# Chunk 0's gate and up projections with the tokens stationary on centred x, and merged DMA transposes, in a fused state-space and SwiGLU kernel

## The chip, the cores and the metric

The kernel runs on one core of one Trainium2 chip. The metric is device microseconds of one launch: 181.08 us, the median of three runs (180.85 to 181.24). Engines: TensorE (PE, with its weight loads PEld), VectorE (DVE), ScalarE (ACT), GpSimd (POOL), SyncE (SP, which here only issues DMAs; SPq is its queue).

## What is computed

The input x has 2048 tokens of 512 features, in bf16. It is layer-normalised, and two branches work on the result:

```python
xn = layernorm(x)                                       # over the 512 features, eps 1e-5
# A: diagonal complex state space, 512 states
Bu = xn @ B_bar.T                                       # B_bar = ((Lam_bar - 1) / Lam) * B
h[t] = Lam_bar * h[t-1] + Bu[t]
A = 2 * real(h @ C.T) + xn * Dskip
# B: SwiGLU, 1376 hidden
B = (silu(xn @ w_gate) * (xn @ w_up)) @ w_down
out = x + A + B
```

## The kernel before

Tokens go in four chunks of 512 (`CW`), each of four tiles of 128; hidden columns in ten tiles of 128 and one of 96 (`FT` = 11). Every matmul of the projections has weights stationary and the transposed, normalised input `xnT` (features on partitions, 512 tokens) moving, four feature blocks (`KD`) per product. All engines run their instructions in the order in which the program writes them (`manual_schedule`), so the order is set by hand: TensorE's stream is written out, and DVE's and ACT's pieces of the state-space work stand in a backlog of (cost, operation) pairs from which `pump(us)` takes what fits beside the matmuls just written; `need(tag)` flushes a stage. A wait of one instruction holds all that stand behind it on its engine, and on SyncE's queue too.

**Head** (lines 120 to 154 loads, 612 to 659). SyncE loads x tile 0, halves of the first gate group, x tile 2, halves of the up group, x tile 3, and so on; ACT's queue loads x tile 1. Weights come in three groups of hidden tiles, 3, 4 and 3 (`fgroups`, line 89). Ten dummy matmuls of 512 columns on a zeroed tile keep TensorE busy meanwhile. Each x tile of chunk 0 goes through statistics on DVE (`ln_stats`, 182), rstd by Ln and Exp on ACT (193), normalising on DVE (`norm_dve`, 205), four transposes on TensorE and a copy from PSUM (`xT_pe`, 215), and then `head_mm` (603) makes three gate and three up tiles for those 128 tokens at once, with 128 moving columns. After the last x tile the parameters of the state space follow: a transpose, exponentials on ACT, a table load, and small sines (`params_a`, `params_a2`, `params_sin`).

**Chunk 0, rest.** Hidden tiles 3 to 6 (line 700), the B projection of the state space (`bproj_tile`, 347; `BT` holds B transposed), hidden tiles 7 to 10. Meanwhile DVE computes statistics and normalised tiles of chunk 1 and sine and cosine tables (`table_ops`, 257). Later chunks get `xnT` by a DMA transpose of each normalised tile (`xT_dma`, 225: 128x512 each). B and C are transposed by DMAs of 128 columns, eight each (lines 139 and 723).

**A chunk in general.** `bproj_chunk(c)`, `gateup_chunk(c)`; ACT drains PSUM (`gu_out` with silu, line 441, and copy, 442; the B projection's copy, 354), DVE multiplies gate and up in pairs (446), rotates, scans (394) and rotates back to `wt`, and computes `CF` from C (338); `out_chunk(c)` has 44 matmuls with w_down (514) and 32 with `CF` (524) into the same banks. Eight PSUM banks go round. `out_chunk(0)` comes after chunk 2's B projection, and so on; the last chunk's results leave through DVE and SyncE (527).

Of the kernel before, what the change touches and what calls it, by code (L numbers as in the profile page):

```python
# [10 lines left out]
F32 = mybir.dt.float32  # L11
# [12 lines left out]
def kernel(  # L24
# [62 lines left out]
    xnT = const.tile([128, KD, L], BF16, name="xnT")  # L87

    fgroups = [(0, 3), (3, 7), (7, FT - 1)]
# [26 lines left out]
    def load_w1_half(tiles, view, gi, k0, k1):  # L116
        a, b = fgroups[gi]
        nc.sync.dma_start(out=tiles[gi][:, k0:k1, :], in_=view[:, k0:k1, a * 128:min(F, b * 128)])  # L118

    nc.sync.dma_start(out=xall[:, 0, :], in_=x_v[:, 0, :])  # L120
    nc.vector.memset(xall[:, 1, 0:2], 0.0)
    nc.scalar.dma_start(out=xall[:, 1, :], in_=x_v[:, 1, :])
# [8 lines left out]
    load_w1(nc.sync, wu_g, wu_v, 1)  # L131
# [5 lines left out]
    for part, src in enumerate((A_B_re, A_B_im)):  # L137
        for k in range(KD):
            nc.sync.dma_start_transpose(out=BT[:, part, k, :], in_=src[:, k * 128:(k + 1) * 128])
        if part == 0:  # L140
            load_w1(nc.sync, wg_g, wg_v, 2)
            load_w1(nc.sync, wu_g, wu_v, 2)

    nc.sync.dma_start(out=w_last[:, :, 0:LB], in_=wg_v[:, :, FL + LA:F])
    nc.sync.dma_start(out=w_last[:, :, LB:LB + LA], in_=wg_v[:, :, FL:FL + LA])
    nc.sync.dma_start(out=w_last[:, :, LB + LA:128], in_=wu_v[:, :, FL:FL + LA])

    def load_late():
        nc.sync.dma_start(out=wu_last[:], in_=wu_v[:, :, FL + LA:F])
        nc.sync.dma_start(out=xall[:, 2 * TPC:NT, :], in_=x_v[:, 2 * TPC:NT, :])  # L150
        nc.sync.dma_start(out=wd_sb[:, 0:nfull, :], in_=B_w_down[0:nfull * 128, :].rearrange("(k p) d -> p k d", p=128))
        if nfull < FT:
            nc.sync.dma_start(out=wd_sb[0:LB, nfull, :], in_=B_w_down[FL + LA:F, :])
            nc.sync.dma_start(out=wd_sb[LB:LB + LA, nfull, :], in_=B_w_down[FL:FL + LA, :])
# [9 lines left out]
    nc.vector.memset(eps_t[:], EPS)
    ident = const.tile([128, 128], BF16, name="ident")
    make_identity(nc, ident[:])
# [24 lines left out]
    lnv = const.tile([128, TPC], F32, name="lnv")  # L191

    def ln_rstd_act(n):
        nc.scalar.activation(out=lnv[:, n:n + 1], in_=mv[:, n, 1:2], func=ACT.Ln, bias=eps_t[:])
        nc.scalar.activation(out=rstd[:, n:n + 1], in_=lnv[:, n:n + 1], func=ACT.Exp, scale=-0.5)

# [8 lines left out]
    def norm_dve(n, lo=0, hi=D):  # L205
        c, i = divmod(n, TPC)
        nc.vector.tensor_scalar(out=xn_tile(c)[:, i, lo:hi], in0=xall[:, n, lo:hi], scalar1=mv[:, n, 0:1],  # L207
                                scalar2=rstd[:, n:n + 1], op0=ALU.subtract, op1=ALU.mult)

    def norm_act(n):  # L210
        c, i = divmod(n, TPC)
        nc.scalar.activation(out=xn_tile(c)[:, i, :], in_=xall[:, n, :], func=ACT.Identity,
                             scale=rstd[:, n:n + 1], bias=nb[:, n:n + 1])

    def xT_pe(n, k0=0, k1=KD, on_dve=False):
        c, i = divmod(n, TPC)
        tp = bank((128, KD, 128), BF16)
        for k in range(k0, k1):
            nc.tensor.transpose(out=tp[:, k, :], in_=xn_tile(c)[:, i, k * 128:(k + 1) * 128], identity=ident[:])  # L219
        if on_dve:  # L220
            nc.vector.tensor_copy(out=xnT[:, k0:k1, n * 128:(n + 1) * 128], in_=tp[:, k0:k1, :])
        else:
            nc.scalar.copy(out=xnT[:, k0:k1, n * 128:(n + 1) * 128], in_=tp[:, k0:k1, :])

    def xT_dma(n):
        c, i = divmod(n, TPC)
        nc.sync.dma_start_transpose(out=xnT[:, :, n * 128:(n + 1) * 128], in_=xn_tile(c)[:, i, :])


# [12 lines left out]
    def prm_transpose():  # L242
        pp = bank((128, 128), BF16)
        nc.tensor.transpose(out=pp[:], in_=prm_rows[:], identity=ident[:])
        return pp

    def params_a(pp):
        V.tensor_copy(out=prm[:].rearrange("p t q -> p (t q)"), in_=pp[:, 0:3 * NQ])
        nc.scalar.activation(out=dt_t[:], in_=ldt, func=ACT.Exp)

    def params_a2():
        V.tensor_tensor(out=dre[:], in0=dt_t[:], in1=lre, op=ALU.mult)
        nc.scalar.activation(out=r_t[:], in_=dre[:], func=ACT.Exp)
        nc.scalar.preload_act_table_set("silu_and_others")
# [529 lines left out]
```

## Time and profile before

| | us |
|---|---|
| median of three runs | 181.08 |
| lowest and highest | 180.85, 181.24 |
| profiled execution | 181.21 |
| its span, first to last instruction | 179.4 |
| granted TensorE clock in it | 0.999 |

The span is 1.8 us shorter than the time of the same execution. Rows of the timeline read: start, duration (both us), engine, line, operation, what it writes `<-` what it reads, count, and in brackets the idle time before it and what ended that. In a merged row the duration covers all of its instructions, and a matmul's end is modelled with the array's latency, so spacings are read from starts. Rows of groups read: busy us, mean ns of one. In tables of stretches the columns are the length, the busy time of PE, PEld, DVE, ACT and POOL, the granted clock, the DMA engines' busy share and GB/s.

### The profile page before, as it was taken

The page shows a single profiled execution, that of the slowest core. Times are in us where ns is not written, and L with a number is a line of the kernel's source. Part 1 is how long each engine was busy: PE and PEld are TensorE (multiplying, and loading weights), DVE is VectorE, ACT ScalarE, POOL GpSimd, SP SyncE. Part 2 cuts the span into 40 slices and gives each one's busy share as a digit, 9 for nine tenths or more (in the row PEclk, how much of TensorE's full clock was granted, in tenths as well). Part 3 has the DMA queues.
Part 4 walks back from the last instruction along what each step waited for, and adds up shares of the span by engine and source line. Part 5 has one row for each costly group of instructions (what it writes and reads, how often), then busy time and mean ns, then how long its engine had stood idle before and what let it go on. Part 6 is the DMA issues. An engine that isn't in the chain of part 4 may idle for free.

```text
span 179.4 us, 2491 instructions
## 1 busy us (share of the span) xinstructions
PE 173.4 (97%) x908; PEld 83.4 (46%) x924; DVE 155.0 (86%) x248; ACT 104.8 (58%) x190; POOL 23.4 (13%) x30
## 2 busy tenths in 40 slices
PE   7899999999999999999999999999999999999993
PEld 2684444443444444444444444444444444444742
DVE  3649998799999999999999999999999986996033
ACT  3459956998299959022799661024866949805000
POOL 7001100000500000025400000014000004315000
PEclk9999999999999999999999999999999999999999
DMA  5999757994036600011840000007300007964512
GB/s 147 294 263 210 163 98 177 357 190 109 5 72 168 252 4 0 0 11 22 112 93 2 0 0 4 0 0 80 37 0 5 0 0 109 139 103 45 76 58 61
DMA packets 28492, 15.53 MB, mean 87 GB/s; under 512 B 18336, under 2 KB 28416, under 8 KB 28448
## 3 DMA queue, kind: packets, MB, share of 16 engines
q1 hardware_dynamic: 24592, 11.87, 28.5%
q0 software_dynamic: 3456, 3.28, 14.4%
q10 hardware_dynamic: 432, 0.23, 0.4%
q8 instruction: 7, 0.11, 0.3%
q14 instruction: 5, 0.04, 0.1%
HBM read 8.03 MB, written 5.24 MB: 74 GB/s over the span
## 4 chain that ended last, share of the span: by engine, by line
PE 93%; DMA 2%; SPq 1%; DVE 1%; issue 1%
PE ps L427 36%; PE ps L514 21%; PE ps L352 15%; PE ps L524 15%; DMA xall<-in_A_x_dram 2%; PE ps L609 2%; PE ps L453 2%; PE ps L463 1%; SPq L118 1%; DVE stats L183 0%; PE ps L219 0%; SPq L126 0%; SPq L120 0%; DVE xn L207 0%; DVE xall L527 0%
## 5 line engine op out<-in xcount | busy, mean ns | idle before, releaser
L514 PE MATMUL ps<-wd_sb,guT 128*128 128x512 bf16 (+4 forms) x195 | 38.6, 355 | 0.2
L427 PE MATMUL ps<-xnT,wg 128*128 128x512 bf16 x143 | 37.6, 379 | 0.3
L427 PE MATMUL ps<-xnT,wu 128*128 128x512 bf16 x146 | 37.5, 379 | 0.1
L394 DVE TENSOR_TENSOR_SCAN g<-r_t,car,u 128x512 bf16<-128x512 f32 x24 | 28.9, 1263 | 0.0
L524 PE MATMUL ps<-CF,wt 128*128 128x512 bf16 (+2 forms) x140 | 28.1, 355 | 0.2
L352 PE MATMUL ps<-xnT,BT 128*128 128x512 bf16 x126 | 28.2, 379 | 0.1
L514 PEld LDWEIGHTS <-guT 128*128 128x128 bf16 (+1 forms) x198 | 18.5, 98 | 19.9
L441 ACT ACTIVATE guT<-ps 128x512 bf16<-128x512 f32 x40 | 25.2, 629 | 2.5 <-PE ps L427 2.3
L442 ACT CAST u<-ps 128x512 bf16<-128x512 f32 x40 | 24.7, 618 | 2.7 <-PE ps L427 2.7
L427 PEld LDWEIGHTS <-wu 128*128 128x128 bf16 x148 | 14.5, 98 | 17.5
L427 PEld LDWEIGHTS <-wg 128*128 128x128 bf16 x148 | 14.3, 98 | 17.6 <-issue 0.8
L530 ACT CAST res<-ps 128x512 bf16<-128x512 f32 x12 | 6.8, 582 | 23.5 <-PE ps L524 23.5
L524 PEld LDWEIGHTS <-wt 128*128 128x128 bf16 x144 | 13.4, 98 | 14.3
L531 POOL DMA_DIRECT2D out_dram<-res x12 | 10.5, 1033 | 72.6 <-ACT res L530 67.5
L352 PEld LDWEIGHTS <-BT 128*128 128x128 bf16 x128 | 12.5, 98 | 15.1
L354 ACT CAST u<-ps 128x512 bf16<-128x512 f32 x32 | 17.7, 614 | 2.4 <-PE ps L352 2.2
L486 ACT ACTIVATE xr<-xall,nb,rstd 128x512 bf16<-128x512 bf16 x16 | 12.0, 808 | 8.4 <-DVE xall L492 5.9
L183 DVE BATCH_NORM_STATS2 stats<-xall 128x6 f32<-128x512 bf16 x16 | 10.7, 671 | 3.2 <-DMA xall<-in_A_x_dram 3.2
L446 DVE TENSOR_TENSOR guT<-guT,u 128x1024 bf16<-128x1024 bf16 x20 | 13.5, 679 | 0.0
L527 DVE TENSOR_TENSOR xall<-ps,xall 128x512 bf16<-128x512 f32 (+2 forms) x6 | 3.1, 514 | 9.1 <-PE ps L524 9.1
L199 POOL TENSOR_TENSOR rstd<-ve,neg_half 128x4 f32<-128x4 f32 x3 | 5.3, 1751 | 43.6 <-DVE ve L198 43.6
L362 DVE TENSOR_TENSOR pm<-u,c 128x2048 bf16<-128x2048 bf16 x8 | 9.8, 1221 | 1.2 <-ACT c L279 1.1
(101 smaller groups left out, 169.0 us busy)
## 6 DMA issues: line engine op xcount, KB each, us to landing
out_dram<-in_A_x_dram SPq DMA_DIRECT2D x1, 1536.0 KB, 8.7
out_dram<-res POOLq DMA_DIRECT2D x12, 128.0 KB, 3.2
out_dram<-xall POOLq DMA_DIRECT2D x3, 512.0 KB, 5.7
wd_sb<-in_B_w_down_dram SPq DMA_DIRECT2D x1, 1280.0 KB, 10.1
xall<-in_A_x_dram SPq DMA_DIRECT2D x1, 1024.0 KB, 5.9
wg<-in_B_w_gate_dram SPq DMA_DIRECT2D x1, 512.0 KB, 6.1
wu<-in_B_w_up_dram SPq DMA_DIRECT2D x1, 512.0 KB, 7.1
xall<-in_A_x_dram SPq DMA_DIRECT2D x1, 512.0 KB, 7.9
```

The costliest lines, as they stand in the source:

```text
L183: nc.vector.bn_stats(out=stats[:, n, 0, :], in_=xall[:, n, :])
L352: nc.tensor.matmul(ps[:], lhsT=BT[:, part, k, q * 128:(q + 1) * 128], rhs=xnT[:, k, c * CW:(c + 1) * CW], start=(k == 0), stop=(k == KD - 1))
L354: nc.scalar.copy(out=u_tiles[c][:, part, q, :], in_=ps[:])
L394: V.tensor_tensor_scan(out=g()[:, part, q, :], data0=r_t[:, q:q + 1].to_broadcast([128, CW]), data1=u_tiles[c][:, part, q, :], initial=ini ...
L427: nc.tensor.matmul(ps[:fs, lo:hi], lhsT=wslice(groups, fi, k), rhs=xnT[:, k, c * CW + lo:c * CW + hi], start=(k == 0), stop=(k == KD - 1))
L441: nc.scalar.activation(out=guT[:fs, fi, :], in_=psg[:fs], func=ACT.Silu)
L442: nc.scalar.copy(out=u_pair[c][:fs, fi % 2, :], in_=psu[:fs])
L446: products.append(lambda: V.tensor_tensor(out=g, in0=g, in1=u, op=ALU.mult))
L486: nc.scalar.activation(out=box["xr"][:], in_=xall[:, n, :], func=ACT.Identity, scale=rstd[:, n:n + 1], bias=nb[:, n:n + 1])
L514: nc.tensor.matmul(o[:], lhsT=gu_tiles[c][:fsz[fi], fi, i * 128:(i + 1) * 128], rhs=wd_sb[:fsz[fi], fi, lo:hi], start=(fi == 0), stop=False)
L524: nc.tensor.matmul(o[:], lhsT=w_tiles[c][:, part, q, i * 128:(i + 1) * 128], rhs=CF[:, part, q, lo:hi], start=False, stop=(part == 1 and q ...
L531: nc.gpsimd.dma_start(out=out_v[:, n, lo:hi], in_=res[:, lo:hi], accum_op=ALU.add)
```

## The change

1. **Chunk 0's gate and up.** Hidden groups are now 4, 4 and 2 tiles. For chunk 0 the tokens are stationary (`xcT`, 128 tokens of centred x, not yet scaled) and the weights move: 512 columns of one group (256 in the last) for one token tile. The row scale rstd comes in the drains (`sw_out`), where tokens are on partitions. The product silu(gate)*up is made token by token in `g0` (in chunk 1's buffer `guT`) and comes to the hidden-major layout by two DMA transposes (`g0_dma`).
2. **Centring.** Tiles 0 and 1 are transposed uncentred by matmuls with the identity, and -mean is added in PSUM by a matmul of a constant matrix (-1/512) with diag(sum of each row); the sums come from DVE (tile 0) and ACT (tile 1). Tiles 2 and 3 are centred on DVE ahead of their transpose. rstd of chunk 0 is a power on POOL, one for each tile; the exponentials of the parameters too. The first ACT table load is gone; silu's comes at the start.
3. **xnT of chunk 0** (only the B projection and the last hidden tile need it) is normalised on DVE and transposed by DMA.
4. **DMA transposes are merged**: one for each chunk's `xnT` (512x512), one for each part of B and of C.
5. **Order.** ACT's queue loads a quarter of the first gate group and half of the first up group. Chunk 1's statistics and normalising stand ahead of most of the tables on DVE; the last hidden tile of chunk 0 comes after its B projection; 4 wide and 3 narrow dummies stand ahead, on a constant of ones that is set at the start.

```diff
-    fgroups = [(0, 3), (3, 7), (7, FT - 1)]
+    fgroups = [(0, 4), (4, 8), (8, FT - 1)]
...
     nc.scalar.dma_start(out=xall[:, 1, :], in_=x_v[:, 1, :])
-    nc.scalar.preload_act_table_set("natural_log_exp_and_others")
-    load_w1_half(wg_g, wg_v, 0, 0, KD // 2)
-    load_w1_half(wg_g, wg_v, 0, KD // 2, KD)
+    load_w1_half(nc.sync, wg_g, wg_v, 0, 0, HK)
+    nc.scalar.preload_act_table_set("silu_and_others")
+    load_w1_half(nc.scalar, wg_g, wg_v, 0, HK, HK + 1)
+    load_w1_half(nc.sync, wg_g, wg_v, 0, HK + 1, KD)
+    load_w1_half(nc.scalar, wu_g, wu_v, 0, 0, HK)
     nc.sync.dma_start(out=xall[:, 2, :], in_=x_v[:, 2, :])
-    load_w1_half(wu_g, wu_v, 0, 0, KD // 2)
-    load_w1_half(wu_g, wu_v, 0, KD // 2, KD)
+    load_w1_half(nc.sync, wu_g, wu_v, 0, HK, KD)
     nc.sync.dma_start(out=xall[:, 3, :], in_=x_v[:, 3, :])
...
-        for k in range(KD):
-            nc.sync.dma_start_transpose(out=BT[:, part, k, :], in_=src[:, k * 128:(k + 1) * 128])
+        nc.sync.dma_start_transpose(out=BT[:, part], in_=src[:, :])
...
+    def diag_dve(i):
+        nc.vector.tensor_scalar(out=diag[:, i, :], in0=ident[:], scalar1=sums[:, i:i + 1], scalar2=None, op0=ALU.mult)
...
+    def cT_mm(ps, src, k, first, stop):
+        nc.tensor.matmul(ps[:, k * 128:(k + 1) * 128], lhsT=src[:, k * 128:(k + 1) * 128], rhs=ident[:], start=first, stop=stop)
+
+    def cT_mean(ps, i, k0, k1):
+        nc.tensor.matmul(ps[:, k0 * 128:k1 * 128], lhsT=minus_mean[:],
+                         rhs=diag[:, i:i + 1, :].to_broadcast([128, k1 - k0, 128]), start=False, stop=True)
...
-    def xT_dma(n):
-        c, i = divmod(n, TPC)
-        nc.sync.dma_start_transpose(out=xnT[:, :, n * 128:(n + 1) * 128], in_=xn_tile(c)[:, i, :])
+    def xT_dma(c):
+        nc.sync.dma_start_transpose(out=runs(xnT[:, c]), in_=xn_tile(c)[:].rearrange("p k i d -> p (k i d)"))
...
+    def sw_mm(ps, groups, gi, i, k0=0, k1=KD):
+        a, b = fgroups[gi]
+        for k in range(k0, k1):
+            nc.tensor.matmul(ps[:, 0:(b - a) * 128], lhsT=xcT[:, k, i * 128:(i + 1) * 128], rhs=groups[gi][:, k, :],
+                             start=(k == 0), stop=(k == KD - 1))
+
+    def sw_out(gi, i, psg, psu):
...
+        nc.scalar.activation(out=g0[:, a:b, i, :], in_=by_k(psg[:, 0:w]), func=ACT.Silu, scale=scale)
+        nc.scalar.activation(out=u_pair[0, gi][:, i % 2, 0:w], in_=psu[:, 0:w], func=ACT.Copy, scale=scale)
...
+    def g0_dma(a, b):
+        nc.sync.dma_start_transpose(out=runs(gu_tiles[0][:, a:b, :]), in_=g0[:, a:b].rearrange("p f i d -> p (f i d)"))
...
-    dummy(10, CW)
-    ln_stats(0)
-    ln_rstd_act(0)
+    dummy(warm, 4, CW)
+    dummy(warm, 3, 128)
+    sum_dve(0)
+    sum_act(1)
+    diag_dve(0)
...
+    head_mm(0, 0)
+    ln_stats(1)
+    mean_act(2)
+    ln_rstd(1, 2)
+    head_mm(0, 1)
+    ln_stats_half(0, 0)
+    center(2, mean2[:])
+    ln_stats_half(0, 1)
+    ln_rstd(0, 1)
+    head_mm(1, 0)
...
+    for n in range(TPC):
+        norm_dve(n)
+    xT_dma(0)
+    params_a()
+    load_bt(1)
+    load_last()
+    load_late()
...
+    need("ln0")
     for part in range(2):
         for q in range(NQ):
             bproj_tile(0, part, q)
...
+    need("ln1")
+    g0_dma(0, fgroups[1][1])
+    g0_dma(fgroups[1][1], FT - 1)
+    load_down()
+    gateup_last(0)
```

`head_mm(which, i)` is gate (0) or up (1) of group 0 for token tile i. In the changed program SyncE's queue is: x tile 0, a gate half and a quarter, x tile 2, an up half, x tile 3, groups 1 and 2, x of chunk 1, B's first transpose, `xnT` of chunk 0, B's second, four small weight loads, x of chunks 2 and 3, `xnT` of chunk 1, the two product transposes (32 and 8 blocks of 128x128), w_down, C's two, `xnT` of chunk 2. Of the DMAs from SyncE and ACT together each waits until the one eight places earlier has landed.

More of the change, by code (lines that the diff above doesn't have):

```diff
@@ L211, in norm_act @@
         c, i = divmod(n, TPC)
-        nc.scalar.activation(out=xn_tile(c)[:, i, :], in_=xall[:, n, :], func=ACT.Identity,
+        nc.scalar.activation(out=xn_tile(c)[:, :, i, :], in_=by_k(xall[:, n, :]), func=ACT.Identity,
                              scale=rstd[:, n:n + 1], bias=nb[:, n:n + 1])
-    def xT_pe(n, k0=0, k1=KD, on_dve=False):
-        c, i = divmod(n, TPC)
[L217 to L223, printed above, removed]
@@ L576, with dummy @@
     BP = 4 * 0.2163
[L577 to L579 removed]
+    one = nc.const_aps.tensor(1.0, (128, 1), BF16)
+    def dummy(ps, n, cols):
         for _ in range(n):
[L581 removed]
+            nc.tensor.matmul(ps[:, 0:cols], lhsT=one.to_broadcast([128, 128]), rhs=one.to_broadcast([128, cols]),
+                             start=True, stop=True)
     def ln_rest(c, on_act):
@@ L593, in one @@
                 (norm_act if on_act else norm_dve)(n)
[L594 removed]
+                if n % TPC == TPC - 1:
+                    xT_dma(c)
             tail.append((0.05 if on_act else 0.35, one))
         return ops, tail
[L600 to L610 removed]
@@ L612 @@
[L612 to L636 removed]
+    G, U = wg_g, wu_g
@@ new lines, in head_mm @@
+    def head_mm(which, i, k0=0, k1=KD):
+        if held[i][which] is None:
+            held[i][which] = bank()
+        sw_mm(held[i][which], (G, U)[which], 0, i, k0, k1)
+    dummy(warm, 4, CW)
[3 more added lines that the diff above has]
+    diag_dve(0)
+    for k in range(KD):
+        cT_mm(p0 if k < HK else p1, xall[:, 0, :], k, k % HK == 0, False)
+    for k in range(KD):
+        cT_mm(p2 if k < HK else p3, xall[:, 1, :], k, k % HK == 0, False)
+    dummy(warm, 1, 128)
+    cT_mean(p0, 0, 0, HK)
```

233 lines of the change are left out of this document (128 added, 105 removed).

## The prediction

> **What bounds the kernel now.** I read the busy shares and the chain first, then the timeline of the first 14 us, then the DMA queue of SyncE (SPq), since the change touches the head and the transfers.
>
> ```profile
> PE 173.4 (97%) x908; PEld 83.4 (46%) x924; DVE 155.0 (86%) x248; ACT 104.8 (58%) x190; POOL 23.4 (13%) x30
> PE 93%; DMA 2%; SPq 1%; DVE 1%; issue 1%
> ```
>
> TensorE is the bound: 97% busy, 93% of the chain. Time can be gained only where it waits, and that is the head. The timeline there:
>
> ```profile
> 1.23 4.19 PE L581 MATMUL ps<-junk 128*128 128x512 bf16 x10 [1.23 <-DVE eps_t L164]
> 3.04 0.69 DVE L183 BATCH_NORM_STATS2 stats<-xall 128x6 f32<-128x512 bf16 x1 [1.85 <-DMA xall<-in_A_x_dram]
> 5.25 0.28 PE L219 MATMUL ps<-ident,xn 128*128 128x128 bf16 x2
> 5.99 0.50 PE L609 MATMUL ps<-xnT,wg 128*128 128x128 bf16 x6 [0.18 <-ACT xnT L223]
> 6.27 0.69 DVE L183 BATCH_NORM_STATS2 stats<-xall 128x6 f32<-128x512 bf16 x1 [0.52 <-DMA xall<-in_A_x_dram]
> 6.83 0.34 PEld L609 LDWEIGHTS <-wu 128*128 128x128 bf16 x6 [0.30 <-DMA wu<-in_B_w_up_dram]
> 8.04 0.69 DVE L183 BATCH_NORM_STATS2 stats<-xall 128x6 f32<-128x512 bf16 x1 [0.86 <-DMA xall<-in_A_x_dram]
> 9.31 0.40 PE L219 MATMUL ps<-ident,xn 128*128 128x128 bf16 x4 [0.63 <-DVE xn L207]
> 10.38 0.83 PE L609 MATMUL ps<-xnT,wg 128*128 128x128 bf16 x12
> 11.04 0.39 PE L219 MATMUL ps<-ident,xn 128*128 128x128 bf16 x4
> 13.28 1.03 PE L427 MATMUL ps<-xnT,wg 128*128 128x512 bf16 x3
> ```
>
> x tile 0 is there at 3.04, the first useful product starts at 5.99, and TensorE then waits for wu (0.30) and for the late x tile 2 (0.63). From 13.28 on it runs without a gap:
>
> ```profile
> 33.14 7.07 PE L352 MATMUL ps<-xnT,BT 128*128 128x512 bf16 x31
> 59.27 7.07 PE L352 MATMUL ps<-xnT,BT 128*128 128x512 bf16 x32
> 66.17 9.68 PE L514 MATMUL ps<-wd_sb,guT 128*128 128x512 bf16 x43
> 75.69 7.07 PE L524 MATMUL ps<-CF,wt 128*128 128x512 bf16 x31
> ```
>
> Thirty-two wide matmuls take 66.17 - 59.27 = 6.90, or 0.216 each; a narrow one (128 columns) takes (11.04 - 10.38)/12 = 0.055. TensorE's streamed columns hardly change: gate and up of chunk 0 stay 80 wide matmuls' worth, the transposes stay 16 narrow ones, and the mean adds four of 256 columns ahead of the first product. So the result is the shift of the head, plus any wait that opens later.
>
> **The head.** By 13.28 the kernel before has made 96 narrow matmuls, the worth of 24 wide ones. The new group 0 is 32 wide ones; the kernel before gets that far at 13.28 + 8 x 0.216 = 15.0. When does the new one (call it H)? The durations:
>
> ```profile
> L223 ACT COPY xnT<-ps 128x256 bf16<-128x256 bf16 x2 | 0.7, 372 | 0.3 <-PE ps L219 0.3
> L212 ACT ACTIVATE xn<-xall,nb,rstd 128x512 bf16<-128x512 bf16 x8 | 6.5, 821 | 6.2 <-DVE nb L202 6.2
> L207 DVE TENSOR_SCALAR xn<-xall,mv,rstd 128x512 bf16<-128x512 bf16 x7 | 2.6, 405 | 0.4 <-ACT rstd L195 0.3
> L199 POOL TENSOR_TENSOR rstd<-ve,neg_half 128x4 f32<-128x4 f32 x3 | 5.3, 1751 | 43.6 <-DVE ve L198 43.6
> ```
>
> The plain sum of tile 0 on DVE isn't in the trace; I price it like the statistics (0.69), bounded by a 512-wide elementwise operation (0.41) and twice the statistics. With the diagonal (0.2, an estimate from the 0.41 row at a quarter of the width), the mean matmul (0.2) and the copy (0.37), half of tile 0 stands at 4.5; ACT's half follows its sum of tile 1 (0.82), its diagonal and its copy, at about 5.1. So data are ready 0.9 sooner than 5.99. Then weights set the pace: they now come in 512-column groups, 1024 KB instead of 768 KB.
>
> ```profile
> 0.00:2.00 2.00, 0.77 (x2) 0.28 (x3) 0.35 (x4) 0.69 (x1) 1.10 (x7) 1.00 0.11 14
> 2.00:4.00 2.00, 2.00 (x6) 0.76 (x5) 0.93 (x3) 0.61 (x2) 1.93 (x5) 1.00 0.93 273
> 4.00:6.00 2.00, 1.82 (x12) 0.84 (x11) 1.61 (x5) 1.41 (x6) 0.15 (x1) 1.00 0.92 232
> 6.00:8.00 2.00, 1.87 (x31) 1.70 (x31) 0.88 (x2) 1.20 (x4) 0.00 (x0) 1.00 1.00 302
> 1.20 0.93 SPq L118 DMA_DIRECT2D wg<-in_B_w_gate_dram  x2
> DMA to landing us min/median/max: 2.7/4.4/6.1
> ```
>
> The GB/s, the last figure of the first four rows, sum to 28, 574, 1038 and 1642 KB at 2, 4, 6 and 8 us. x tile 2 was the end of the first 768 KB, moved by 4.8 and seen at 6.27; x tile 3 the end of 1280 KB, moved by 6.8 and seen at 8.04: 1.2 to 1.4 from move to use. The wu wait ended 1.2 after its 960 KB. The first wg half, issued at 1.20, is the end of 448 KB, moved by 3.5 and landed after 2.7, at 3.9: only 0.4. I take 0.9 and keep 0.4 and 1.4. Group 0's gate is complete after 768 KB (both x tiles and 512): 4.8 + 0.9 = 5.7. Its up halves come at 1280 and 1408 KB: 6.8 and 7.2, plus 0.9. So: gate of tiles 0 and 1 from 5.1, ending 5.7 + 6 x 0.216 = 7.0; up of tile 0 from 7.7, its second half from 8.1, done at 8.55; then 20 wide matmuls (4.3), 8 narrow transposes and the parameters' (0.5), and about 0.25 for tile 3, whose statistics and centring stand behind its landing. **H = 13.6**, a gain of **1.4**. Without any weight wait H = 5.1 + 6.9 + 0.5 = 12.5 (gain 2.5); with 1.4 for landing, 14.0 (gain 1.0).
>
> This lets ACT's queue, which issues a quarter of gate and half of up after its table load, share the engines with SPq; if the transfers went in issue order, the gate's third quarter would come behind 1152 KB and H would be 14.05. [...]
>
> **What is hidden.** Draining by tokens adds a per-row scale to ACT's drains, but 16 wide and 8 half ones are some 13 us (0.6 and 0.4 each) beside 17 us of matmuls. The rstds and both exponentials go to POOL; five stand ahead of the sines, one after the other at up to 1.75, from about 6.2 on: rstd of the last tile at 13 to 14, dt at 14.5 to 16. ACT's sines stand ahead of the drain of tile 2 and hold it till 15.4 to 16.8; TensorE wants that drain's PSUM bank at about 17.5. Hidden; if POOL is slower still, it costs up to 0.5. DVE's backlog begins with the statistics of chunk 1 and reaches CF, which the first state-space outputs need, after 58.4 us:
>
> ```profile
> 13.56 0.68 DVE L183 BATCH_NORM_STATS2 stats<-xall 128x6 f32<-128x512 bf16 x1
> 66.79 4.05 DVE L338 SCALAR_TENSOR_TENSOR CF<-CT,nc2im,cm 128x512 bf16<-128x512 bf16 x6
> 71.17 0.75 DVE L338 SCALAR_TENSOR_TENSOR CF<-CT,nc2im,cm 128x512 bf16<-128x512 bf16 x1 [0.33 <-ACT cm L335]
> ```
>
> The same operations now start after the sines' arguments, at 15.9 to 17.3, so CF ends at 74.3 to 75.7. TensorE will want the eighth CF row at 75.7 (below). Covered, with 0 to 1.4 to spare; what goes beyond is paid in full.
>
> **SyncE's queue decides.** The transposes become fewer instructions but more data: chunk 0's xnT (4 blocks of 128x512) and the product g*u (10 blocks) are new on this queue.
>
> ```profile
> 5.90 7.27 SPq L139 DMA_TRANSPOSE BT<-in_A_B_re_dram  x4
> 15.02 5.09 SPq L139 DMA_TRANSPOSE BT<-in_A_B_im_dram  x4
> 27.79 0.50 SPq L150 DMA_DIRECT2D xall<-in_A_x_dram  x1
> 28.34 0.58 SPq L151 DMA_DIRECT2D wd_sb<-in_B_w_down_dram  x1
> 28.96 2.60 SPq L153 DMA_DIRECT2D wd_sb<-in_B_w_down_dram  x1
> 31.61 0.57 SPq L154 DMA_DIRECT2D wd_sb<-in_B_w_down_dram  x1
> 32.23 6.43 SPq L723 DMA_TRANSPOSE CT<-in_A_C_re_dram  x4
> L227 SPq DMA_TRANSPOSE xnT<-xn x12: 1188/1219/1283, 21.9 to 91.5; - x12
> DMA to landing us min/median/max: 2.4/2.4/3.7
> ```
>
> A block costs SyncE 1.22 and lands 1.2 after its issue ends. No row shows a merged one. Call M the price of four blocks in one instruction: 1.2 if all of it is per instruction, 4.9 if all is per block. Plain DMAs of 1024 and 1280 KB take 0.50 and 0.58, so I take 0.5 of the 1.22 as fixed and 0.72 per block: M = 0.5 + 4 x 0.72 = **3.4**, and keep both ends. [...]
>
> - xnT of chunk 1: BT's first transpose can't start before the last up half is there (8.5) and then waits for room as before (7.27 - 5.09 = 2.2). Behind it come xnT of chunk 0, BT's second, five small loads (2.7) and xnT of chunk 1: landed at 8.5 + 2.2 + 4M + 2.7 + 1.2 = 14.6 + 4M, that is 28.2, or 4.6 after DVE has normalised chunk 1 (26.3 to 27.5 by my count of its queue): 30.9 to 32.1. TensorE wants it at H + 6.9 (group 1) + 3.5 (group 2) + 6.9 (B projection) + 0.9 = 31.8. Just in time; in the kernel before this point is 33.14.
> - xnT of chunk 2: after that the ten product blocks (2.5M), the three wd loads (0.58 + 2.60 + 0.57, 3.8), CT (2M, and 1.2 of waiting as in its row) and itself: landed at 19.6 + 9.5M = 51.9. ACT's normalising of chunk 2 must end by 53; by its place behind four drains of chunk 1 it ends at about 50. Wanted at 31.8 + 6.9 + 1.8 + 17.3 = 57.8, against 59.27 before. The first state-space output follows at 57.8 + 6.9 + 9.5 = 74.2 (before: 75.69), the eighth CF row 1.5 later.
>
> **The sum.** Head 1.4 earlier, all else in TensorE's order unchanged: 181.21 of the profiled execution (span 179.4 and 1.8 around it) - 1.4 = 179.8. That execution lies 0.13 above the median of the three runs, 181.08, so I say **179.7**.
>
> **The rivals.**
> - *The transposes are dear (slower).* M from 4.2 on: xnT of chunk 2 then lands after 59.5, more than 1.5 behind its need, and all of the gain is gone. At M = 4.9 it lands at 66.2, a wait of 8.4: 181.1 - 1.4 + 8.4 = 188. For it: in the trace every block costs 1.2 alike, from HBM or SBUF. Against: plain DMAs show a fixed part. Chance 0.24.
> - *The clock opens later.* Ten dummies at 0.42 each, then 0.055 for 128 columns (cold would be 0.105): in this trace the clock opened after some 4 us of dense work, by 5.25. The new kernel gives it 2 us of dummies and then transposes with gaps. If it needs another stretch of that length, gate of tiles 0 and 1 runs at 0.42: done at 8.65 instead of 7.0, and up begins then, not at 7.7: 1.0 lost, 180.7. Chance 0.09. [...]
> - *DVE or POOL runs late.* POOL operations above 1.75 push the sines, DVE's backlog and CF behind their cover: 0.5 to 1.0 lost, 180.2 to 180.7. Chance 0.10.
> - *The weights come at once.* Gain 2.5, then held at about 2.4 by xnT of chunk 1: 178.6. Chance 0.07.
> - The forecast, 178.9 to 180.4: chance 0.50.
>
> A difference below 0.2% (0.36 us) can't be told from none in a measurement of this kernel. Faster: 0.50 + 0.07, and 0.10 of the two middle rivals: 0.67; within: 0.09; slower: 0.24. The range goes from 178.4, below the fastest case, to 183.0, into the dear transposes, and leaves out some 0.17 of theirs and little below.
>
> **What would show it.** First matmul from xcT at about 5.1, group 0 done by 13.6; matmuls of 512 columns 0.216 apart from there; no wait of TensorE ahead of the B projections of chunks 1 and 2; a merged 512x512 transpose near 3.4 on SyncE; CF done by 75.7. I am wrong if SyncE shows more than 4.2 for it, if TensorE is still at half clock after 6, or if gate and up weights land after 9.

## The result and the profile after

| | before | after |
|---|---|---|
| median, us | 180.91 (180.81 to 181.24, 8 runs) | **179.94** (179.04 to 180.57, 8 runs) |
| ratio, 95% interval | | 0.9941 (0.9915 to 0.9966) |
| profiled execution, its span | 181.21, 179.4 | 179.48, 177.5 |
| group 0 of chunk 0 done (before: 32 wide matmuls' worth) | 15.0 | 13.40 |
| B projection of chunks 1, 2 starts | 33.14, 59.27 | 31.57, 57.70 |
| first state-space output | 75.69 | 74.12 |

The change is faster by 0.6%. Its median falls into a gap: four of the eight times lie at 179.04 to 179.59, four at 180.28 to 180.57, and the profile is of the lower four. The shares and the chain of the page of after, as for before:

```profile
PE 172.8 (97%) x852; PEld 82.1 (46%) x868; DVE 157.7 (89%) x258; ACT 109.2 (61%) x188; POOL 26.7 (15%) x36
PE 92%; DMA 3%; DVE 1%; SPq 1%; issue 1%; ACT 0%
```

TensorE is the bound as before. Its timeline, first the head and then the later stages (start, duration, what it does):

```profile
0.78 2.19 PE L644 MATMUL ps<-const-bfloat16-1.0 128*128 128x512 bf16 x7 [0.78 <-PEq L857]
3.23 1.04 PE L255 MATMUL ps<-ident,xall 128*128 128x128 bf16 x8 [0.26 <-DMA xall<-in_A_x_dram]
5.23 2.21 PE L492 MATMUL ps<-wg,CF 128*128 128x512 bf16 x8
7.28 1.13 PE L492 MATMUL ps<-wu,CF 128*128 128x512 bf16 x4
10.09 0.40 PE L255 MATMUL ps<-ident,CF 128*128 128x128 bf16 x4 [0.16 <-DVE ve L205]
13.40 1.03 PE L492 MATMUL ps<-wg,CF 128*128 128x512 bf16 x4
...
31.57 7.07 PE L390 MATMUL ps<-xnT,BT 128*128 128x512 bf16 x31
57.70 7.07 PE L390 MATMUL ps<-xnT,BT 128*128 128x512 bf16 x32
...
74.12 2.10 PE L587 MATMUL ps<-CF,wt 128*128 128x512 bf16 x9
```

The reader is to see three things. The first product starts at 5.23 where it was 5.99, and group 0 is done at 13.40, where the gate of group 1 begins. From there to the first state-space output nothing is won or lost: 59.27 - 57.70 and 75.69 - 74.12 are both 1.57. (The two executions differ by 1.73; the other 0.16 comes later and isn't traced.) And TensorE's last wait in the head is the one at 10.09, ahead of tile 3's transposes. The chain of work that ended last says what it waits for (start, duration, what):

```profile
2.16 4.76 DMA xall<-in_A_x_dram
6.95 0.73 ACT xnT L236 x2
7.71 0.35 DVE CF L246
...
8.83 0.61 DVE stats L196
...
9.68 0.35 DVE CF L246
```

This is x tile 2. It lands just before 6.95, ScalarE sums its rows (line 236) and VectorE centres it (line 246). In VectorE's order the rest of tile 0's statistics (8.06 to 8.83) and only then the statistics and the centring of tile 3 come behind that, so tile 3's start at 8.8, though x tile 3 has landed at 8.2. Group 0's end comes 6.45 after ScalarE's start on tile 2. SyncE's queue in the same execution:

```profile
8.50 5.75 SPq L149 DMA_TRANSPOSE BT<-in_A_B_re_dram  x1
14.37 1.75 SPq L268 DMA_TRANSPOSE xnT<-CF  x1
16.16 3.68 SPq L149 DMA_TRANSPOSE BT<-in_A_B_im_dram  x1
22.17 0.51 SPq L161 DMA_DIRECT2D xall<-in_A_x_dram  x1
24.14 4.51 SPq L268 DMA_TRANSPOSE xnT<-xn  x1
...
48.87 1.96 SPq L268 DMA_TRANSPOSE xnT<-xn  x1
```

A merged 512x512 transpose takes the queue 1.75 or 1.96 from SBUF, 3.68 from HBM, and 4.51 where it stands behind the 1 MB load of line 161. POOL's powers, and two places of DVE's queue:

```profile
6.78 0.58 POOL L206 TENSOR_TENSOR rstd<-ve,neg_half 128x1 f32<-128x1 f32 x1 [3.24 <-DVE ve L205]
11.70 1.08 POOL L288 TENSOR_TENSOR dt_t<-e_t,prm 128x4 f32<-128x4 f32 x1
15.60 0.68 DVE L196 BATCH_NORM_STATS2 stats<-xall 128x6 f32<-128x512 bf16 x1
66.05 5.39 DVE L376 SCALAR_TENSOR_TENSOR CF<-CT,nc2im,cm 128x512 bf16<-128x512 bf16 x8
```

The row at 15.60 is the first of chunk 1's statistics. The eight CF rows end at 71.4, 4.2 ahead of the eighth's use (74.12 and 1.5).

### The profile page after: what moved, and what is told of

Read it like the earlier page. It is cut to its first block, busy times and chain, and to the rows that moved or that the text cites. A ratio compares the mean times of both kernels' runs of the same rounds, so it can differ in the third digit from the quotient of the medians.

```text
span 177.5 us, 2367 instructions
## 1 busy us (share of the span) xinstructions
PE 172.8 (97%) x852; PEld 82.1 (46%) x868; DVE 157.7 (89%) x258; ACT 109.2 (61%) x188; POOL 26.7 (15%) x36
## 3 DMA queue, kind: packets, MB, share of 16 engines
q0 software_dynamic: 3456, 3.28, 14.5%
## 4 chain that ended last, share of the span: by engine, by line
PE 92%; DMA 3%; DVE 1%; SPq 1%; issue 1%; ACT 0%
PE ps L465 29%; PE ps L577 21%; PE ps L390 16%; PE ps L587 15%; PE ps L492 8%; DMA xall<-in_A_x_dram 3%; PE ps L516 2%; PE ps L526 1%; SPq L118 0%; ACT xnT L236 0%; DVE CF L246 0%; DVE stats L196 0%; SPq L124 0%; PE ps L255 0%; DVE stats L200 0%
## 5 line engine op out<-in xcount | busy, mean ns | idle before, releaser
L465 PE MATMUL ps<-xnT,wg 128*128 128x512 bf16 x120 | 30.8, 380 | 0.1
L465 PE MATMUL ps<-xnT,wu 128*128 128x512 bf16 x114 | 30.0, 379 | 0.2
L392 ACT CAST u<-ps 128x512 bf16<-128x512 f32 x32 | 17.9, 592 | 5.6 <-PE ps L390 5.6
L479 ACT ACTIVATE guT<-ps 128x512 bf16<-128x512 f32 x30 | 17.9, 596 | 5.2 <-PE ps L465 5.1
L480 ACT CAST u<-ps 128x512 bf16<-128x512 f32 x30 | 17.5, 585 | 5.1 <-PE ps L465 4.8
L465 PEld LDWEIGHTS <-wu 128*128 128x128 bf16 x120 | 11.8, 98 | 14.1
L465 PEld LDWEIGHTS <-wg 128*128 128x128 bf16 x120 | 11.6, 98 | 14.5 <-issue 0.8
L492 PEld LDWEIGHTS <-CF 128*128 128x128 bf16 x96 | 9.2, 98 | 8.0 <-issue 0.7
L492 PE MATMUL ps<-wg,CF 128*128 128x512 bf16 (+1 forms) x48 | 10.9, 348 | 0.0
L206 POOL TENSOR_TENSOR rstd<-ve,neg_half 128x1 f32<-128x1 f32 (+1 forms) x7 | 6.9, 984 | 26.8 <-DVE ve L205 26.8
L492 PE MATMUL ps<-wu,CF 128*128 128x512 bf16 (+1 forms) x47 | 10.7, 343 | 0.1
L196 DVE BATCH_NORM_STATS2 stats<-xall 128x6 f32<-128x512 bf16 x15 | 10.1, 672 | 0.0
```

Source lines behind the costliest of these rows:

```text
L196: nc.vector.bn_stats(out=stats[:, n, 0, :], in_=xall[:, n, :])
L392: nc.scalar.copy(out=u_tiles[c][:, part, q, :], in_=ps[:])
L465: nc.tensor.matmul(ps[:fs, lo:hi], lhsT=wslice(groups, fi, k), rhs=xnT[:, c, k, lo:hi], start=(k == 0), stop=(k == KD - 1))
L479: nc.scalar.activation(out=guT[:fs, fi, :], in_=psg[:fs], func=ACT.Silu)
L480: nc.scalar.copy(out=u_pair[c][:fs, fi % 2, :], in_=psu[:fs])
L492: nc.tensor.matmul(ps[:, 0:(b - a) * 128], lhsT=xcT[:, k, i * 128:(i + 1) * 128], rhs=groups[gi][:, k, :], start=(k == 0), stop=(k == KD - 1))
```

## The experiments

No kernel leaves out any of the computation. Ratios are to the kernel before on the same chip. "Group 0's end" is the start of the first matmul of group 1.

**The changed kernel again, unaltered.**

> The changed kernel unaltered, once more. Its first eight times fall in two groups, 179.0 to 179.6 and 180.3 to 180.6. [...] Theory 3 (chance of one session): one group only.

Measured: 179.31 (179.09 to 180.00), ratio 0.9912 (0.9898 to 0.9926). Its timeline of TensorE:

```profile
4.99 2.59 PE L492 MATMUL ps<-wg,CF 128*128 128x512 bf16 x8
13.18 1.03 PE L492 MATMUL ps<-wg,CF 128*128 128x512 bf16 x4
```

The first four wide matmuls start 0.42 apart and the later ones 0.215: TensorE ran at half pace until about 6.4, where in the first profile it was until 5.65. Yet group 0 ends earlier, at 13.18. Half pace up to there cost nothing that shows, since TensorE, by the starts of its matmuls, still waits for tile 3, if only for 0.07: ScalarE starts on x tile 2 at 6.73, and 13.18 is 6.45 later, as in the first profile. The upper group of times didn't come again (five times up to 179.56, one of 180.00), as theory 3 has it; what made it in the first eight was not tested.

**Every merged transpose cut into pieces of 128x512.**

```diff
-        nc.sync.dma_start_transpose(out=runs(xnT[:, c]), in_=xn_tile(c)[:].rearrange("p k i d -> p (k i d)"))
+        for k in range(KD):
+            nc.sync.dma_start_transpose(out=runs(xnT[:, c, k:k + 1]), in_=xn_tile(c)[:, k].rearrange("p i d -> p (i d)"))
```

and likewise for B, C and the products.

> The changed kernel with each merged DMA transpose cut into pieces of 128x512 (4 for each xnT, 4 for each half of B and C, 10 for the product). Theory (a piece costs SyncE 1.22, as before the change, so the queue decides): xnT of chunk 1 lands at about 34 to 35 and TensorE waits 2.5 to 3.5 ahead of that B projection, then up to 5 more ahead of chunk 2's: 184 to 188 us. Rival (SyncE's queue has room either way and merging is worth nothing here): 179 to 180.6, no wait of TensorE over 0.3 ahead of the B projections.

Measured: 191.20 (189.93 to 191.90), ratio 1.0541 (1.0512 to 1.0569). What TensorE waited for in all, and rows of its timeline:

```profile
PE ps L392 <- DMA xnT<-xn: 6.9, 5, 3.2
```
```profile
34.97 8.96 PE L392 MATMUL ps<-xnT,BT 128*128 128x512 bf16 x32 [3.23 <-DMA xnT<-xn]
68.19 8.60 PE L392 MATMUL ps<-xnT,BT 128*128 128x512 bf16 x29 [0.71 <-DMA xnT<-xn]
```

In the table of stretches the granted clock (the third figure from the end) is below 1 in both places:

```profile
30.00:50.00 20.00, 16.59 (x71) 6.40 (x70) 14.42 (x36) 14.16 (x25) 2.50 (x2) 0.91 0.72 150
60.00:80.00 20.00, 16.38 (x63) 6.46 (x62) 12.57 (x20) 9.96 (x18) 0.00 (x0) 0.83 0.41 119
```

Waits make 6.9, one of 3.23 ahead of chunk 1's B projection and four of 0.71 to 1.09 ahead of and inside chunk 2's, and slow matmuls follow both: 32 take 8.96 where they took 7.07 in after. The clock's share is 0.09 and 0.17 of 20, that is 1.8 and 3.4; with the waits 12.1 of the 12.4 by which this execution (191.90) is longer than after's. So the mechanism of the rival "the transposes are dear" is real: with this queue the tokens-stationary form needs the merging. It came out dearer than 188, because the waits also let TensorE's clock go down.

**The kernel before with B and C merged, and nothing else.**

```diff
-        for k in range(KD):
-            nc.sync.dma_start_transpose(out=BT[:, part, k, :], in_=src[:, k * 128:(k + 1) * 128])
+        nc.sync.dma_start_transpose(out=BT[:, part], in_=src[:, :])
```

and likewise for C.

> The kernel before with B's and C's DMA transposes merged (two each instead of eight each) and nothing else changed. Theory (TensorE's wait is in the head, ahead of what these transposes feed): within 0.2 us of the kernel before, 180.7 to 181.3. Rival (merging frees the DMA engines or SyncE for the head's loads): faster by 0.3 or more.

Measured: 181.27 (180.51 to 181.78), ratio 1.0012 (1.0000 to 1.0025). Merging alone gains nothing: B's two parts take SyncE's queue 6.86 and 4.17 where they took 7.27 and 5.09, and that queue wasn't the bound.

**Tiles 0 and 1 centred on DVE, like tiles 2 and 3.** The sums, diagonals and mean matmuls go, and two narrow dummies between them.

```diff
-    sum_dve(0)
-    sum_act(1)
-    diag_dve(0)
...
+    for i, p in enumerate((p0, p2)):
+        ln_stats(i)
+        center(i, mv[:, i, 0:1])
+        for k in range(KD):
+            cT_mm(p, xc[:, i, :], k, k == 0, k == KD - 1)
+        cT_copy(nc.scalar.copy, p, i)
```

> The changed kernel, but tiles 0 and 1 are centred on DVE from their statistics ahead of the transpose, as tiles 2 and 3 are; no sums, diagonal and mean matmuls. Theory (weights set the pace of the head): tile 0 is ready within 0.3 of the changed kernel, the fourth gate matmul still waits for its weights, and the time is within 0.3 us of the changed kernel's. Rival (the early centring in PSUM is what brings the gain): the first product starts 0.5 or more later, group 0 ends later by as much, 180 to 180.5 beside 179.5.

Measured: 181.49 (180.54 to 181.98), ratio 1.0017 (0.9999 to 1.0034): the whole gain is gone. But the timeline shows two causes at once:

```profile
4.32 0.61 PE L255 MATMUL ps<-ident,CF 128*128 128x128 bf16 x4 [1.35 <-DVE CF L246]
5.93 3.62 PE L492 MATMUL ps<-wg,CF 128*128 128x512 bf16 x8
15.40 1.03 PE L492 MATMUL ps<-wg,CF 128*128 128x512 bf16 x4
```

The first product is 0.7 late (5.93), and with TensorE idle for 1.35 the eight gate matmuls take 3.4 from the first start to the next row at 9.34, at half pace: the clock opened only at about 10.1. The next kernel tells the two apart.

**The same, with TensorE kept busy**: three more wide dummies ahead, two between the tiles.

```diff
     dummy(warm, 4, CW)
+    dummy(warm, 3, CW)
     dummy(warm, 3, 128)
...
         cT_copy(nc.scalar.copy, p, i)
+        if i == 0:
+            dummy(warm, 2, CW)
```

> Tiles 0 and 1 are centred on VectorE from their full statistics, as in the run before it of that kind, but TensorE is kept busy: three more wide dummy matmuls ahead of tile 0's transposes (0.43 each, so busy to about 4.26) and two between the transposes of tiles 0 and 1 (to about 5.6). That run lost 2.2 us to the changed kernel: 0.7 by a first product at 5.93, and the rest, by theory, by a clock that opened only at 10.0, after an idle stretch of 1.35. Theory (the clock was the larger part; centring in PSUM itself is worth little): the clock opens by 6.5, first product at 5.9 to 6.0, group 0 done at 13.4 to 14.0, time 179.4 to 180.1. Rival (the later centred tiles themselves cost it, by VectorE's and ScalarE's later work): clock early all the same, group 0 done at 15 or later, 181.0 or more.

Measured: 179.35 (179.19 to 179.69), ratio 0.9917 (0.9899 to 0.9935).

```profile
5.73 1.94 PE L492 MATMUL ps<-wg,CF 128*128 128x512 bf16 x8
13.26 1.03 PE L492 MATMUL ps<-wg,CF 128*128 128x512 bf16 x4
```

The theory holds. Centring in PSUM brings the first product from 5.73 to 5.0 to 5.2, and that earned nothing here; what it does is keep TensorE busy, and dummies do that as well. One thing differs besides: with the statistics of tiles 0 and 1 done ahead, less stands on VectorE behind tile 2, and group 0 ends 6.00 after ScalarE's start on tile 2 (7.26), not 6.45.

**No dummies at the start, and nine wide ones.**

```diff
-    dummy(warm, 4, CW)
-    dummy(warm, 3, 128)
```
```diff
-    dummy(warm, 4, CW)
-    dummy(warm, 3, 128)
+    dummy(warm, 9, CW)
```

> The changed kernel without the seven dummy matmuls at its start. TensorE's first work is then tile 0's transposes at 3.0. Theory (the clock opens 4.9 to 5.6 after TensorE becomes busy, as it did from 0.78): it opens at 7.9 to 8.6; from 5.0 to there some 8 wide matmuls run at 0.42 where 15 could have, 1.5 to 1.8 lost, of which the weights' lateness (group 0 ended 0.9 after the earliest that 32 wide matmuls from 5.0 allow) hides about half: group 0 done at 14.0 to 14.6, time 180.0 to 181.0. Rival (the weights alone pace group 0 whatever the clock does): within 0.3 of the changed kernel, 179.2 to 179.9.

> The changed kernel with nine wide dummy matmuls at its start in place of four wide and three narrow ones: TensorE is busy without a gap from 0.78 to about 4.6, so tile 0's transposes start at 4.6 and not at 3.0, and the first product at about 5.9. Theory (clock and weights set the pace together): the clock opens at 5.3 to 6.0 in every execution, the later first product costs 0 to 0.5, and the times lie closer together than those of the changed kernel (179.0 to 180.6): 179.3 to 179.9, no single one above 180.2. Rival (a spread that comes from the transfers): as wide a spread as the changed kernel's, single times up to 180.6.

Measured: without, 180.18 (179.65 to 181.78), ratio 0.9962 (0.9940 to 0.9984); with nine, 179.79 (179.54 to 180.24), ratio 0.9941 (0.9922 to 0.9961). Timelines, first without, then with nine:

```profile
4.93 3.62 PE L492 MATMUL ps<-wg,CF 128*128 128x512 bf16 x8
14.36 0.81 PE L492 MATMUL ps<-wg,CF 128*128 128x512 bf16 x3
```
```profile
4.57 0.70 PE L255 MATMUL ps<-ident,xall 128*128 128x128 bf16 x8
5.96 1.90 PE L492 MATMUL ps<-wg,CF 128*128 128x512 bf16 x8
13.61 1.03 PE L492 MATMUL ps<-wg,CF 128*128 128x512 bf16 x4
```

Without them the clock opened at about 9 (by the spacing of the matmuls, and later than the 7.9 to 8.6 of the theory), and group 0 ended at 14.36: 1.0 to 1.2 later than in the first two profiles of the changed kernel. The theory's numbers for that end and for the time hold. Nine make the clock open by 4.8, but the first product comes at 5.96: no gain. Group 0's end is again 6.45 after ScalarE's start on tile 2 (7.16). One of the six times was above the 180.2 that I had allowed, and the spread (0.7) is little narrower than the 0.9 of the unaltered kernel's second lot.

**Group 0's weights all by SyncE's queue.**

```diff
-    load_w1_half(nc.scalar, wg_g, wg_v, 0, HK, HK + 1)
-    load_w1_half(nc.sync, wg_g, wg_v, 0, HK + 1, KD)
-    load_w1_half(nc.scalar, wu_g, wu_v, 0, 0, HK)
+    load_w1_half(nc.sync, wg_g, wg_v, 0, HK, KD)
     nc.sync.dma_start(out=xall[:, 2, :], in_=x_v[:, 2, :])
+    load_w1_half(nc.sync, wu_g, wu_v, 0, 0, HK)
```

> The changed kernel with group 0's weights all issued from SyncE's queue in the order of the kernel before; none goes by ScalarE's queue. Theory (the second queue lets the first halves land side by side, and group 0 is paced by weights): the up weights' first half lands 0.5 to 0.8 later, group 0 done 0.3 to 0.6 later, time 179.7 to 180.2. Rival (the bytes, not the queue, set the landing): within 0.2 of the changed kernel, 179.2 to 179.7; ScalarE, freed of two issues, could even give back 0.1.

Measured: 179.57 (179.37 to 179.62), ratio 0.9924 (0.9905 to 0.9943). My theory was wrong: group 0 ended at 13.03, earlier than in any run so far. The time lies in the rival's range, but not for the rival's reason: it came out 0.4 above what that end gives in the other runs, and the timeline has a wait ahead of chunk 1's B projection:

```profile
31.54 7.08 PE L389 MATMUL ps<-xnT,BT 128*128 128x512 bf16 x32 [0.18 <-DMA xnT<-xn]
```

The idle time is counted from a modelled end; by starts the wait is 0.34. The transpose of chunk 1's x was issued at 23.51, behind the 1 MB load, and landed 8.0 later. The next limit, right behind group 0, is that transfer.

**The 1 MB load of x behind chunk 1's transpose**, alone and with the weights on one queue; and the changed kernel again on the same chip.

```diff
                     xT_dma(c)
+                    if c == 1:
+                        load_late()
...
     load_last()
-    load_late()
```

> The changed kernel with one load moved: the 1 MB of x of chunks 2 and 3 is issued right behind chunk 1's merged transpose, not 1.5 to 2 ahead of it. In the runs so far that transpose landed 6.5 to 8.0 after its issue at 23.5 to 24.1, at 30.4 to 31.5, and chunk 1's B projection begins at 31.3 to 31.6. Theory (the transpose stands behind that load, and it is a second limit right behind group 0's end): it lands 4.3 to 5 after its issue, at 28 to 29, and chunk 1 has 2.5 to spare; the median moves by 0 to 0.3 at most, since group 0's end still sets the time (179.1 to 179.5), but the late single times of 180 to 180.6 vanish if they came from there. Rival (the transpose takes its 6.5 to 8 by itself): landing as before, times as before.

> Both moves together: group 0's weights all on SyncE's queue (group 0 then ended at 13.03, but chunk 1's B projection waited for its transposed x at 31.54 and the time was 179.57), and the 1 MB load of x behind chunk 1's transpose. In the runs without a wait the profiled time is group 0's end and 166.1 (166.08 to 166.11 in five of them). Theory (the wait at 31.54 took what the earlier group 0 gave): no wait there, 13.03 and 166.1 make 179.1, median 178.9 to 179.3, below the changed kernel beside it by 0.1 to 0.4. Rival (the weights on one queue cost something else later): 179.5 to 179.7 again.

> The changed kernel unaltered, to stand beside the other three on one chip, and for the spread of its single times (179.04 to 180.57 in the first eight, in two groups; 179.09 to 180.0 in six later ones). Theory (the spread comes from where TensorE's clock opens, 5.65 in one profile and 6.4 in another, and from chunk 1's transposed x): 179.2 to 179.9, with single times up to 180.6 possible. If all lie within 179.0 to 179.6, the group at 180.3 to 180.6 belonged to its chip or hour and isn't explained by these runs.

Measured: load moved 179.59 (179.04 to 179.90), ratio 0.9923 (0.9902 to 0.9945); both moves **179.09** (178.82 to 179.50), ratio 0.9906 (0.9882 to 0.9929); unaltered 179.86 (179.32 to 180.22), ratio 0.9941 (0.9919 to 0.9962). Timelines of the first, SyncE and TensorE:

```profile
24.55 1.80 SPq L268 DMA_TRANSPOSE xnT<-xn  x1
```
```profile
5.03 0.82 PE L492 MATMUL ps<-wg,CF 128*128 128x512 bf16 x3
6.63 1.24 PE L492 MATMUL ps<-wg,CF 128*128 128x512 bf16 x5 [0.78 <-DMA wg<-in_B_w_gate_dram]
13.80 1.03 PE L492 MATMUL ps<-wg,CF 128*128 128x512 bf16 x4
```

of both moves:

```profile
5.04 1.90 PE L491 MATMUL ps<-wg,CF 128*128 128x512 bf16 x8
12.73 1.03 PE L491 MATMUL ps<-wg,CF 128*128 128x512 bf16 x4
```

and of the unaltered one:

```profile
6.60 1.35 PE L492 MATMUL ps<-wg,CF 128*128 128x512 bf16 x5
13.68 1.03 PE L492 MATMUL ps<-wg,CF 128*128 128x512 bf16 x4
```

The moved load frees the transpose: 1.80 of queue, landing about 4.5 after its issue. But it doesn't move the median by what could be told here, since group 0's end decides; so the spread isn't from there. The pair "load moved" and "both moves" is the cleanest of the study: the same chip, the clock open by the first product in both (5.03 and 5.04), and group 0's end at 13.80 and 12.73. With ScalarE's queue in use TensorE waits for the gate's last quarter until 6.63; with one queue it starts on it at 5.70. What closes the head with two queues is x tile 2, though: ScalarE starts on it at 7.35, 6.45 ahead of 13.80. With one queue it is there 1.1 sooner, and TensorE no longer waits for tile 3:

```profile
6.21 0.63 ACT L235 ACTIVATE xnT<-xall 128x512 bf16<-128x512 bf16 x1 [0.71 <-DMA xall<-in_A_x_dram]
```

So the second queue, a part of the change, costs instead of gaining: 1.1 between these two executions, of which the first is the slowest of its six, and 0.50 between the medians, whose intervals overlap. The version with both moves is faster than the kernel before; than the unaltered change its median is lower by 0.77, though these two intervals overlap as well.

**Chunk 1's normalisation behind the first pair of tables.**

```diff
-    queue("tables", tables[1:2])
+    queue("tables", tables[1:5])
     queue("ln1", norm1)
-    queue("tables", tables[2:])
+    queue("tables", tables[5:])
```

> The changed kernel with chunk 1's normalisation behind the whole first pair of tables on VectorE instead of ahead of it (the part of the change that put it ahead is undone in part: three table instructions, 2.6, and some products go first). The norm then ends at about 27.4 instead of 24.1. Theory (the transpose's landing is held by the 1 MB load ahead of it, which lands at 28.5 or so): the transpose issued at 27.4 lands at 31.5 to 32.2, TensorE waits 0 to 0.7 for it, time 179.3 to 180.1. Rival (the landing follows the norm by 6.5 to 8): landing at 34 to 35.4, a wait of 2.5 to 4 at 31.5, and if that closes TensorE's clock as the waits of the unmerged kernel did, 4 more: 182 to 187.

Measured: 179.84 (179.60 to 180.05), ratio 0.9942 (0.9922 to 0.9962). SyncE and TensorE:

```profile
27.51 1.77 SPq L268 DMA_TRANSPOSE xnT<-xn  x1
```
```profile
30.82 1.03 PE L516 MATMUL ps<-xnT,w_last 128*128 128x512 bf16 x4
31.91 4.28 PE L390 MATMUL ps<-xnT,BT 128*128 128x512 bf16 x18
```

The theory holds: issued 3.4 later than in after, it lands in time but for 0.2 (30.82 and four matmuls of 0.216 make 31.68, not 31.91). The load ahead of it, not the norm, set its landing. Normalising ahead of the tables is worth about 0.2 here.

## Why the prediction was right

All profiles of the changed kernel and its variants. "Tile 2" is ScalarE's start on x tile 2, "behind it" what lies from there to group 0's end; the last column is time less end. The forecast of 179.7 lies, like the median of 179.94, in the gap between the two groups of the first eight times, so that the two came so close is in part luck.

| kernel | tile 2 | group 0's end | behind it | time of that execution | difference |
|---|---|---|---|---|---|
| after | 6.95 | 13.40 | 6.45 | 179.48 | 166.08 |
| unaltered, 2nd | 6.73 | 13.18 | 6.45 | 179.27 | 166.09 |
| unaltered, 3rd | 7.23 | 13.68 | 6.45 | 179.78 | 166.10 |
| load moved | 7.35 | 13.80 | 6.45 | 179.90 | 166.10 |
| nine dummies | 7.16 | 13.61 | 6.45 | 179.69 | 166.08 |
| norm behind the tables | 7.06 | 13.51 | 6.45 | 179.82 | 166.31, 0.2 of it the wait at 31.9 |
| unmerged | 6.63 | 13.08 | 6.45 | 191.90 | 178.82, the waits above |
| centred on DVE, with dummies | 7.26 | 13.26 | 6.00 | 179.37 | 166.11 |
| centred on DVE | 7.59 | 15.40 | 7.81 | 181.50 | 166.10 |
| no dummies | 7.00 | 14.36 | 7.36 | 180.45 | 166.09 |
| both moves | 6.21 | 12.73 | 6.52 | 178.90 | 166.17 |
| weights on one queue | 6.08 | 13.03 | 6.95 | 179.55 | 166.52, 0.34 of it the wait at 31.5 |

- **"The result is the shift of the head, plus any wait that opens later."** Right. Over 2.7 us of shift the time is group 0's end and 166.1 to 166.2, and what stands above that is a wait that the timeline shows. The kernel before fits too: 181.21 - 15.0 = 166.2.
- **H = 13.6, a gain of 1.4.** Measured 13.18 to 13.68 in three profiles of the unaltered kernel, so the step holds; that the size came out so well is in part luck. The sum has weights set the pace and adds 0.25 for tile 3, whose statistics and centring "stand behind its landing". The weights' terms were off against each other. The gate was to be complete at 5.7; its last quarter landed at 6.2, 5.8 and 6.6 in the three. The up halves were to come at 7.7 and 8.1; in after up started at 7.28 and its second half at 7.82. And in all three it is the wait for tile 3 that decides, and that stands behind x tile 2, to which the sum gives no landing at all. In seven of the twelve profiles group 0's end comes 6.45 after ScalarE's start on tile 2, wherever the clock opened (from 4.8 with nine dummies to about 6.9 in the third unaltered one) and whenever the gate's last quarter landed (5.5 to 6.6). In the other five TensorE has no wait ahead of tile 3: two are held by the half clock and two have tile 2 early, while centred with dummies has less behind it.
- **The second queue.** SyncE's 128 KB and ScalarE's 256 KB, issued at 1.65 and 1.80, moved side by side. The list of DMA issues up to 12 us of after has them with their times to landing:

```profile
wu<-in_B_w_up_dram ACTq DMA_DIRECT2D x1, 256.0 KB, 5.3
wg<-in_B_w_gate_dram SPq DMA_DIRECT2D x1, 128.0 KB, 4.5
```

  So the gate's quarter landed at 6.2 and x tile 2, issued next on SyncE, at 6.9, just ahead of the up half that is wanted later (7.1). The 13.6 takes it that the two queues share the DMA engines, for which the prediction has no row; in after they did: x tile 2, issued 0.36 later than ScalarE's 256 KB, landed ahead of it, and from 3.5 to 6.0 SyncE's queue (q1) had 47.7% and ScalarE's (q10) 50.3% of the engines' time. That sharing harms here I didn't see: I shared out the up weights but let the gate's 768 KB come first all the same. With one queue x tile 2 was there at 6.08 and 6.21, with two at 6.63 to 7.59 in ten profiles; and the up half itself came no later with one (6.67 and 6.74) than in nine of those ten (6.90 to 7.80). The 14.05 for issue order doesn't follow from the sum's own terms: a third quarter at 1152 KB is there at 7.3, and what is left behind it makes 14.2 or more.
- **"Data are ready 0.9 sooner."** They were (5.23 against 5.99, 0.8), but it earned nothing: the kernel with the first product at 5.73 is as fast. The reading of the kernel before was off as well: its wait until 9.31 isn't for a late x tile 2. VectorE's statistics of tile 3, which wait for x tile 3 until 8.04, stand ahead of tile 2's normalising (8.87). From that 8.04 to 15.0 are 7.0; in after the chain begins at 6.95 and takes 6.45. So of the 1.6 that the head gained, 1.1 is the earlier x tile and 0.5 the shorter way behind it.
- **The rival "the clock opens later": 1.0, giving 180.7.** The price was right: with the clock open at 9 (no dummies) group 0 ends about 1.0 later, profiled time 180.45, median 180.18. In the unaltered kernel it opens at 5.65 to 6.9, where the wait for tile 3 hides it.
- **What is hidden.** Right in sign, wrong in size. A power on one column takes POOL 0.58 and the exponential 1.08, not up to 1.75, so dt was done at 12.8 and not at 14.5 to 16. VectorE's backlog did begin late, at 15.60, near the 15.9 of the sum, and still CF ended at 71.4 where I had 74.3 to 75.7. The step that failed is that the later start goes through to CF in full: from there to CF's end VectorE took 55.8 (before: 58.4 from 13.56), with 1.3 less work and 1.2 less idle time between. The rival "DVE or POOL runs late" never was near.
- **M = 3.4.** Measured 1.75 to 1.96 from SBUF without a load ahead, 3.68 from HBM, 4.51 behind the 1 MB load. The term stood for all of them alike: it was about right for B and C, which come from HBM, and too large for xnT. The chance of 0.24 for dear transposes was too much by these rows, though the mechanism is real: unmerged, 191.2.
- **Signs of being wrong that came and cost nothing.** SyncE did show more than 4.2 for a merged transpose (4.51, and 5.75 for B's first, where its second took 3.68), and TensorE was at half clock after 6 in the second and third profile of the unaltered kernel. Neither reached the time: 4.51 is time in the queue behind the load, and the transpose landed at 31.2, before its use at 31.6; the half clock is hidden as said above.
- **xnT of chunk 1 at 30.9 to 32.1, wanted at 31.8: "just in time".** Right in the sum: in the three unaltered profiles it landed at 30.4 to 31.2, wanted at 31.4 to 31.9. Wrong in the cause: I had it follow the norm by 4.6. The norm was over at 24.1, not at 26.3 to 27.5, and it was the 1 MB load in front that held the transpose. xnT of chunk 2, issued at 48.87, was never in question.

What stays open: the first eight times of the changed kernel lie in two groups, 179.04 to 179.59 and 180.28 to 180.57, and no profile of the unaltered kernel is from the upper one. By the sum above it would have group 0's end at 14.2 to 14.5, as late as without dummies. An x tile 2 that lands at 7.7 to 8.0 could make that, or a late clock together with late weights; no run shows it. No run isolates the tokens-stationary form by itself either, and none moves the work that stands on VectorE between tile 2's centring and tile 3's.

## What to carry to other kernels

When one engine is busy without a gap from some point on, measure that point and the constant behind it: each edit then has to move the point or open a wait later, and one row tells which. To find what sets the point, follow the chain that ended last back through every engine, and see whether the distance stays the same over several executions: here the weights looked like the limit, and it was an x tile two engines away. Before a slow variant is put down to the operation that was changed, look at the spacing of the matmuls: taking work away from TensorE at the start can cost more through its clock than the work itself (here 181.49 with TensorE idle between the tiles, 179.35 with dummies in the place of the work). And a second DMA queue needn't bring anything sooner: here it let a later need move beside an earlier one, and the x tile that closes the head came 0.4 to 1.5 later in these executions than with one queue.

## What the runs showed of the hardware

- TensorE's clock, read from the spacing of wide matmuls (0.42 at first, 0.215 from some point on), opens at different times for the same code: at 5.65, at 6.4 and at about 6.9 in the three profiles of the changed kernel, and by 4.8 in the kernel with nine dummies, each with its first matmul at 0.78. That is 4.0 to 6.1 after it became busy.
- The granted clock of the stretches doesn't show this phase at the start, though it shows the one in the middle of the unmerged kernel (0.91 and 0.83). A row of the kernel without dummies, where wide matmuls stand 0.42 apart (four of them in 1 us), has 1.00 in the column behind the five engines. In the trace of after the clock's first record starts only at 5.64, where the spacing changes, and the column takes the time without a record as full. The row:

```profile
7.00:8.00 1.00, 1.00 (x4) 0.38 (x3) 0.24 (x1) 0.72 (x2) 0.05 (x1) 1.00 1.05 367
```

- In the middle of the unmerged kernel a single wait of 3.23 was enough to slow the matmuls behind it (8.96 for 32, where after has 7.07; granted clock 0.91 over those 20 us). So were four waits of 0.71 to 1.09 with one matmul between each two (8.60 for 29; 0.83).
- A merged DMA transpose of 512x512 costs SyncE 1.75 to 1.96 from SBUF in after. A piece of 128x512 costs 1.22 in the kernel before, which makes 4.9 for four. Behind the 1 MB load it is 4.51 for the merged one and 5.63 for four pieces in the unmerged kernel.
